# A two-stage attention kernel on one core: order of the first loads, staging of the weights, and projections of the first batch summed pair by pair

## The chip, the core and the metric

The kernel runs on one core of a Trainium2 chip. The engines are PE (TensorE, matrix products), DVE (VectorE), ACT (ScalarE), POOL (GpSimd) and SP (SyncE, which here only issues transfers). Each engine works through its own list of instructions in the order in which the program was written out, and waits at an instruction until what it needs is there. Times are device microseconds (us) of one execution, from the first to the last instruction plus what lies around them.

## What is computed

For 8 batches with 8 heads, 576 positions and head size 64, the reference adds two attentions and feeds the sum to a gated attention over four experts:

```
q_d, k_d, v_d = means over 4 neighbouring positions
out_up = repeat(softmax(scale * q_d @ k_d.T) @ v_d, 4)
scores = where(|i - j| < 4, scale * q @ k.T, -1e9)
x = out_up + softmax(scores) @ v              # (8, 576, 512)
logits = x @ w_gate ; keep the best 2 of 4 experts, softmax over them -> w
for e in range(4):
    q, k, v = x @ wq[e], x @ wk[e], x @ wv[e]
    ye = causal_softmax(scale * q @ k.T) @ v @ wo[e]
    out += w[e] * ye
```

## The kernel before

**Stages.** Heads are taken in pairs, four pairs to a batch, 32 pairs in all; pair 0 is the first of batch 0. Stage 1 makes x for one pair. Pair by pair it loads `lq`, `lk`, `lr` (v in rows of four positions) and `lv` (v in windows, two halves). PE makes the banded scores `sc` and the small scores `scd`. DVE masks (`lp`), takes the maximum, POOL subtracts it (L494; for a few pairs, list `LU`, ACT does this inside ten exponentials), ACT takes the exponential, DVE sums and inverts, POOL normalizes (L500). Means of four are `qd` and `kd` (L514, on DVE in batch 0) and `vd` (POOL, from `lr`, L528 and L529). PE transposes (`tp`), multiplies with v (`o`), DVE adds into `x` (L614), ACT rounds it to `xh` (L618), and POOL takes the rest `xl` (L619, and L621 for the last 64 positions).

**Stage 2** projects x of all four pairs: `q` and `k` of two halves of the experts (`pj`, L636) and five tiles of `v` with the gate (`pv`). Each product is three products of rounded parts (high by high, low by high, high by low), so one projection of `q` is, for each of the four pairs, three matmuls of 320 and three of 256 columns, and one tile of `v` is twelve matmuls of 260 columns. All four pairs add into the same sum. **Stage 3** makes scores (`sq`, `sqt`), softmax, transposes (`tq`), the product with v (`o`, L873) and the output product (`po`).

**Weights.** `weights()` loads `wqk` (1 MB), `wvg` (0.5 MB) and `wo` (0.5 MB), each into a staging tile `wst`, and splits them in chunks on ACT (high part, L434) and POOL or DVE (low part, L436). All three staging tiles have one buffer, so each load waits until the one before is split.

**Order.** A planner inside the kernel writes out the order. Every operation has a due time (its unit's place in a cycle of length `CYC`, less a lead by kind, `LEAD` and `OPL`, less `SHIFT`), a cost and its dependences; a model of the engines then takes, engine by engine, what is ready and due first. The order so found is fixed in the program. `WAT` holds the due times of the weights, `LDS` the lead of the loads. Where the model sees PE too idle, it puts in filler matmuls on constants (`wu`, `wub`, L444) that keep PE's clock up. 14 such matmuls (`NW0`) open the program.

Sums live in two pools of PSUM: two large buffers (`big`: `sc`, `o1`, `pj`, `po`, `sqt`) and four small ones (`tr`: `scd`, `tp`, `pv`, `sq`, `tq`).

In the model every projection depends on one object `WTS`, which stands for all the weights together:

```
xs = [(XH[b, c], 0) for c in range(NP)] + [XL[b, c] for c in range(NP)] + [WTS]
op(kind, "T", dense(12, 320), lambda: mm(0, 320), r=xs, w=[ps], alloc=[ps] + alloc)
```

Of the kernel before, what the change touches and what calls it, by code (L numbers as in the profile page):

```python
# [57 lines left out]
class Plan:  # L58
# [44 lines left out]
    def schedule(self):  # L103
# [17 lines left out]
        idle_at = dict(zip("TVAGD", (1069 + 427.0 * NW0, 4300.0, 2000.0, 1500.0, 300.0)))  # L121
# [162 lines left out]
SWM = {None: 16.3, "quarter": 14.0, "column": 36.7, "row": 12.3}  # L284
# [15 lines left out]
LAT = {"T": 200.0, "V": 130.0, "A": 150.0, "G": 150.0, "D": 2250.0}  # L300
# [15 lines left out]
def tile_attn_then_moe(ctx: ExitStack, tc: tile.TileContext, qT, kT, v, wqk, wvg, wo, out):  # L316
# [108 lines left out]
    def weights():  # L425
        for at, (src, n, m, whi, wlo) in zip(WAT, ((wqk, NP, 512, wqk_h, wqk_l), (wvg, NP, 260, wvg_h, wvg_l),
                                                   (wo, 2, D, wo_h, wo_l))):
            plan.now = at
            st = buf(wk, [128, n, m], "wst", NPA, tag="pta")
            op("wld", "D", 1500 if m == 260 else 2900, lambda st=st, src=src: nc.sync.dma_start(  # L430
                st(), src.rearrange("(c p) j -> p c j", p=128)), w=[st], alloc=[st])
            for c in range(n):
# [5 lines left out]
                   r=[(st, c)], w=[(WTS, key)])  # L438

# [12 lines left out]
    def load(b, c):  # L452
# [4 lines left out]
        op("load", "D", 830, lambda: nc.sync.dma_start(q(), qT[b, c]), w=[q], alloc=[q])  # L457
        op("load", "D", 830, lambda: nc.sync.dma_start(k(), kT[b, c]), w=[k], alloc=[k])
        op("load", "D", 830, lambda: nc.sync.dma_start(vr(), bass.AP(
            tensor=v.tensor, offset=v.offset + ((b * NP + c) * SP + PADL) * 128,  # L460
            ap=[[512, WD], [WD * 512, 2], [128, 4], [1, 128]])), w=[vr], alloc=[vr])
        for x, r in enumerate(halves):
            op("load", "D", 450, lambda x=x, r=r: nc.sync.dma_start(vw()[r], bass.AP(
                tensor=v.tensor, offset=v.offset + ((b * NP + c) * SP + SH * x) * 128,
                ap=[[128, W], [TQ * 128, 5], [1, 128]])), w=[(vw, x)], alloc=[] if x else [vw])

    def s1_local(b, c):
# [13 lines left out]
        op("local", "T", 600, mm, r=[q, k], w=[sc], alloc=[sc, p])  # L481
# [22 lines left out]
    def s1_down(b, c):  # L504
# [34 lines left out]
        op("down", "T", 500, mm, r=[qd, kd], w=scs, alloc=scs + [p])  # L539
# [28 lines left out]
    def s1_out(b, c):  # L568
# [60 lines left out]
    def project(kind, b, p, w0, alloc):  # L629
# [42 lines left out]
    def s2_v(b, t):  # L672
# [73 lines left out]
    def s2_scores(b, p, i):  # L746
# [15 lines left out]
        op("scores", "T", dense(3, n) + 20, mm, r=[q, k], w=pss, alloc=pss + [pr])  # L762
# [266 lines left out]
```

## Time and profile before

| | |
|---|---|
| runs: median (lowest to highest, 3 runs) | 541.54 us (540.61 to 543.1) |
| profiled execution, its span | 543.61 us, 541.8 us |
| PE busy | 515.7 us (95%) |
| DVE busy | 421.2 us (78%) |
| ACT busy | 330.5 us (61%) |
| POOL busy | 291.0 us (54%) |
| mean granted PE clock | 0.981 |

The span runs from the first to the last instruction. PE busy includes the fillers. The shares are averages over the whole run; the first 60 us look quite different from the rest.

### The profile page before, as it was taken

To read this page: it belongs to the slowest core of one execution; us is meant where nothing else is said; L and a number is where in the kernel's file an instruction comes from. 1 tells how busy PE (TensorE), PEld (TensorE's weight loads), DVE (VectorE), ACT (ScalarE), POOL (GpSimd) and SP (SyncE) were. 2 spreads that over 40 slices of the span, in tenths; PEclk is the share of its full clock that TensorE was granted. 3 is DMA by queue.
4 is the path that set the end of the run, shared out by engine and by line. 5 is a ranking of instruction groups with operands and counts; after the bars stand their busy time and mean duration, and the time that the engine had idled before them with its cause. 6 is when DMAs were issued, how large, how long until landed. Compare 5 with 4: busy or idle time off the path is not lost.

```text
span 541.8 us, 17296 instructions
## 1 busy us (share of the span) xinstructions
PE 515.7 (95%) x6870; PEld 453.5 (84%) x6872; DVE 421.2 (78%) x1256; ACT 330.5 (61%) x995; POOL 291.0 (54%) x360
## 2 busy tenths in 40 slices
PE   7596998999899999999999999999999999999998
PEld 3374898888789888999889998999988989998877
DVE  6597778879977879888789878896897796637871
ACT  1594663666556665676656566775665665545773
POOL 3397985737444656676534546865663653312220
PEclk8798999899999999999999999999999999999999
DMA  9868542603142323614144332632333010200112
GB/s 198 236 152 221 142 113 73 148 23 100 50 135 90 93 57 92 218 48 136 30 138 122 97 80 79 211 93 69 104 90 126 13 36 2 88 2 10 45 45 89
DMA packets 43585, 52.78 MB, mean 97 GB/s; under 512 B 3312, under 2 KB 26352, under 8 KB 43504
## 3 DMA queue, kind: packets, MB, share of 16 engines
q1 hardware_dynamic: 43504, 51.67, 34.0%
q8 instruction: 54, 0.88, 0.7%
q14 instruction: 27, 0.22, 0.1%
HBM read 41.16 MB, written 9.44 MB: 93 GB/s over the span
## 4 chain that ended last, share of the span: by engine, by line
PE 68%; DVE 14%; DMA 8%; ACT 4%; POOL 3%; issue 2%; SPq 1%; POOLq 0%; DVEq 0%; ACTq 0%
PE pj L636 14%; PE tq L827 7%; PE po L890 7%; PE o L873 7%; PE pv L681 7%; PE sq L761 6%; PE tp L578 6%; DMA lk<-in_kT_dram 4%; PE sc L479 3%; PE o L593 3%; PE o L607 2%; PE sqt L791 2%; DMA lq<-in_qT_dram 2%; PE scd L537 2%; DVE pr L776 1%
## 5 line engine op out<-in xcount | busy, mean ns | idle before, releaser
L767 ACT ACTIVATE pr<-pr,pst 128x512 f32<-128x512 f32 (+3 forms) x128 | 70.9, 555 | 27.1 <-DVE pst L769 25.6
L776 POOL TENSOR_SCALAR pr<-pr,pst,gw 128x256 f32<-128x256 f32 (+3 forms) x66 | 45.5, 692 | 66.3 <-DVE pst L774 34.3
L636 PE MATMUL pj<-xh,wqk_h 128*128 128x320 f32 (+1 forms) x256 | 79.6, 311 | 0.0
L636 PE MATMUL pj<-xl,wqk_h 128*128 128x320 f32 (+1 forms) x256 | 75.5, 295 | 0.0
L636 PE MATMUL pj<-xh,wqk_l 128*128 128x320 f32 (+1 forms) x256 | 75.4, 295 | 0.0
L769 DVE CUSTOM_DVE_ANT_0 pr<-sq,causal 128x512 f32<-128x512 f32 (+3 forms) x128 | 57.5, 484 | 11.2 <-PE sq L761 10.8
L827 PE MATMUL tq<-ident,pr 128*128 128x128 f32 x400 | 58.7, 276 | 4.7 <-DVE pst L769 1.4
L500 POOL TENSOR_TENSOR lp<-lp,lst 128x640 f32<-128x640 f32 x30 | 38.6, 1287 | 33.7 <-DVE lst L499 23.6
L827 PEld LDWEIGHTS tq<-ident,pr 128*128 128x128 f32 x400 | 45.3, 141 | 10.1 <-POOL pr L776 2.6
L636 PEld LDWEIGHTS pj<-xh,wqk_h 128*128 128x128 f32 x256 | 48.3, 189 | 1.3 <-issue 0.4
L636 PEld LDWEIGHTS pj<-xh,wqk_l 128*128 128x128 f32 x256 | 48.3, 189 | 0.0
L636 PEld LDWEIGHTS pj<-xl,wqk_h 128*128 128x128 f32 x256 | 48.1, 188 | 0.0
L549 ACT ACTIVATE dp<-scd,dst 128x144 f32<-128x144 f32 x96 | 35.2, 375 | 16.3 <-DVE dst L544 14.1
L761 PE MATMUL sq<-k,q 64*128 64x128 f32 (+3 forms) x384 | 43.4, 342 | 0.0
L528 POOL TENSOR_TENSOR lr<-lr 72x512 f32<-72x512 f32 x30 | 38.6, 1286 | 8.0 <-DMA lr<-in_v_dram 8.0
L619 POOL TENSOR_TENSOR xl<-x,xh 128x576 fp32r<-128x576 f32 x29 | 41.1, 1418 | 0.0
L353 DVE COPY pt<-tp 128x256 f32<-128x256 f32 (+2 forms) x64 | 31.8, 509 | 10.4 <-PE tp L578 10.1
L593 PE MATMUL o<-pt,lv 64*64 64x58 f32 (+1 forms) x1280 | 36.8, 229 | 2.2 <-DVE pst L793 1.8
L681 PE MATMUL pv<-wvg_h,xh 128*128 128x260 f32 x128 | 38.2, 298 | 0.0
L776 DVE TENSOR_SCALAR pr<-pr,pst,gw 128x256 f32<-128x256 f32 (+3 forms) x62 | 36.5, 593 | 0.7
L494 POOL TENSOR_TENSOR lp<-lp,lst 128x640 f32<-128x640 f32 x24 | 30.8, 1285 | 10.6 <-DVE lst L485 7.6
L890 PE MATMUL po<-oh,wo_h 128*128 128x320 f32 (+1 forms) x112 | 36.1, 322 | 0.3 <-DVE lp L482 0.3
(154 smaller groups left out, 1503.7 us busy)
## 6 DMA issues: line engine op xcount, KB each, us to landing
lv<-in_v_dram SPq DMA_DIRECT2D x64, 160.0 KB
lq<-in_qT_dram SPq DMA_DIRECT2D x32, 292.0 KB
lk<-in_kT_dram SPq DMA_DIRECT2D x32, 292.0 KB
lr<-in_v_dram SPq DMA_DIRECT2D x32, 288.0 KB
out_dram<-ot SPq DMA_DIRECT2D x28, 288.0 KB
wst<-in_wqk_dram SPq DMA_DIRECT2D x1, 1024.0 KB
out_dram<-ot SPq DMA_DIRECT2D x4, 160.0 KB
wst<-in_wvg_dram SPq DMA_DIRECT2D x1, 520.0 KB
```

What stands on the lines that cost most here:

```text
L500: op("l_nrm", "GV", (pool_tt(n), dve(n)), lambda e: eng[e].tensor_tensor(p(), p(), st[:, :, 2:3].to_broadcast([128, NT, W]), op=OP.mult), ...
L528: G.tensor_tensor(vr()[:, :, 0:2, :], vr()[:, :, 0:2, :], vr()[:, :, 2:4, :], op=OP.add)
L593: T.matmul(o()[r, 512 * x + z:512 * x + z + n], lv()[kr, t, r], pt()[kr, t - k0, at:at + n], start=True, stop=True)
L619: op("xl", "GV", (1360, dve(576)), lambda e: eng[e].tensor_tensor(xl(), x(), xh()[:, 0:S].bitcast(F32), op=OP.subtract), r=[x, (xh, 0)], w ...
L636: T.matmul(ps()[:, H0 + n0:H0 + n1], ww[:, c, w0 + 128 * p:w0 + 128 * p + 128], xx[b, c]()[:, n0:n1], start=(i == 0), stop=(i == 3 * NP - 1))
L681: T.matmul(ps()[:, :260], xx[b, c]()[:, 128 * t:128 * t + 128], ww[:, c, :], start=(i == 0), stop=(i == 3 * NP - 1))
L761: T.matmul(pss[e]()[:m, :n], q()[r, x, qc], k()[r, y, :n], start=one, stop=end)
L767: A.activation(pr()[:, e, :], pr()[:, e, :], AF.Exp, bias=st[:m, e, 4:5], scale=-1.0, accum_out=st[:m, e, 0:1])
L769: op("s_max", "V", dve(n) + 4, lambda e=e, ps=ps: V.tensor_tensor_reduce(pr()[:, e, :], ps()[:m, :n], causal[:, 640 - n:640], -0.125, BIG, ...
L776: op("s_nrm", "GV", (327 + n / 1.2, 189 + n / 1.92), lambda g, e=e: eng[g].tensor_scalar(pr()[:, e, :], pr()[:, e, :], st[:m, e, 3:4], gw( ...
L827: T.transpose(ps()[:, 128 * x:128 * x + 128], pr()[:, c] if i == 4 else pr()[:, e, c], ident)
L890: T.matmul(ps()[:, H0 + n0:H0 + n1], ww[:, p, 128 * c:128 * c + 128], xx[b, p]()[:, n0:n1], start=(i == 0), stop=(i == 5))
```

## The change

It does five things. Loads and weights of the first batch get another order: the loads of all four pairs first, `wvg` next, `wqk` after it, `wo` last (`WAT`, and a later due time `LVL` for the loads of `lv`). Each weight gets a staging buffer of its own, in space whose owner is not in use yet. A projection depends on its own weight, and chunk by chunk where it can. The first `q` projection and two `v` tiles of batch 0 are written as four parts, one for each pair, that add into a sum left open between them. The planner's numbers (due times, leads, some costs) are other ones, which moves instructions all through the program.

```
-CYC = 68.4
+CYC = 66.8
-WAT, NW0 = (36.0, 29.0, 58.0), 14
+WAT, NW0 = (48.0, 21.0, 52.0), 14
-LU, B0 = (1, 3, 8, 10, 16, 25, 26), 1
+LU, B0 = (1, 3, 8, 11, 14, 24, 26, 30), 1
-LDS = 5.8
+LDS, LVL = 5.2, 21.0
+PAIRWISE, NV1 = (("q", 0, 0),), 2
...
-            st = buf(wk, [128, n, m], "wst", NPA, tag="pta")
-            op("wld", "D", 1500 if m == 260 else 2900, lambda st=st, src=src: nc.sync.dma_start(
+            tag, bufs = {id(wqk): ("pta", NPA), id(wvg): ("ptb", NPB), id(wo): ("pr3", NPR[3])}[id(src)]
+            st = buf(wk, [128, n, m], "wst", bufs, tag=tag)
+            op("wld", "D", 2300 if m == 260 else 875 * n, lambda st=st, src=src: nc.sync.dma_start(
...
+    def needs(whi):
+        return [(WTS, (id(whi), c)) for c in range(whi.shape[1])]
...
+        plan.now += LVL
         for x, r in enumerate(halves):
-            op("load", "D", 450, lambda x=x, r=r: nc.sync.dma_start(vw()[r], bass.AP(
+            op("load", "D", 1150, lambda x=x, r=r: nc.sync.dma_start(vw()[r], bass.AP(
...
-        xs = [(XH[b, c], 0) for c in range(NP)] + [XL[b, c] for c in range(NP)] + [WTS]
+        xs = [(XH[b, c], 0) for c in range(NP)] + [XL[b, c] for c in range(NP)] + needs(wqk_h)
...
+    def project_by_pair(kind, b, p, w0, alloc):
+
+        ps = big("pj")
+
+        def mm(c):
+            for n0, n1 in ((0, 320), (320, S)):
+                for i, (ww, xx) in enumerate(((wqk_h, XH), (wqk_l, XH), (wqk_h, XL))):
+                    T.matmul(ps()[:, H0 + n0:H0 + n1], ww[:, c, w0 + 128 * p:w0 + 128 * p + 128], xx[b, c]()[:, n0:n1],
+                             start=(c == 0 and i == 0), stop=(c == NP - 1 and i == 2))
+        for c in range(NP):
+            op(kind, "T", dense(3, 320) + dense(3, 256) + 15, lambda c=c: mm(c), r=[(XH[b, c], 0), XL[b, c]] + needs(wqk_h)[c:c + 1],
+               w=[ps], alloc=[] if c else [ps] + alloc)
+        return ps
...
-            op("v", "T", dense(12, 260), mm, r=[(x, 0) for x in xh] + [XL[b, c] for c in range(NP)] + [WTS], w=[ps],
-               alloc=[ps] + ([vg] if t == 0 else []))
+            parts = [(c,) for c in range(NP)] if b == 0 and t < NV1 else [tuple(range(NP))]
+            for cs in parts:
+                op("v", "T", dense(3 * len(cs), 260) + 15, lambda cs=cs: mm(cs),
+                   r=[(xh[c], 0) for c in cs] + [XL[b, c] for c in cs] + [needs(wvg_h)[c] for c in cs], w=[ps],
+                   alloc=[ps] + ([vg] if t == 0 else []) if cs[0] == 0 else [])
```

What the planner makes of it is seen in the engines' lists. SP issues the transfers one after the other. Before, from its eighth transfer (numbers tell buffers apart; `lv_173` belongs to pair 1, `lq_248` to pair 2):

```order
L463 DMA lv_157<-in_v_dram 64x5x128
L463 DMA lv_173<-in_v_dram 64x5x128
L430 DMA wst_177<-in_wqk_dram 128x4x512
L463 DMA lv_173<-in_v_dram 64x5x128
L457 DMA lq_248<-in_qT_dram 128x584
L458 DMA lk_261<-in_kT_dram 128x584
```

And in the changed kernel from the same place (`lq_212` is pair 2, `lq_284` pair 3):

```order
L471 DMA lv_157<-in_v_dram 64x5x128
L464 DMA lq_212<-in_qT_dram 128x584
L465 DMA lk_241<-in_kT_dram 128x584
L466 DMA lr_257<-in_v_dram 72x2x512
L471 DMA lv_276<-in_v_dram 64x5x128
L464 DMA lq_284<-in_qT_dram 128x584
L465 DMA lk_319<-in_kT_dram 128x584
L466 DMA lr_335<-in_v_dram 72x2x512
```

The 1 MB of `wqk` stood ahead of the loads of pair 2; now those of pairs 2 and 3 come directly, `wvg` is the 17th transfer and `wqk` the 21st.

POOL's list before, around the last pair of batch 0 (`xl_874` is pair 2, `xl_971` pair 3, `lp_534` pair 4):

```order
L619 TENSOR_TENSOR xl_874<-x_745,xh_777 128x576
L500 TENSOR_TENSOR lp_534<-lp_534,lst1_73 128x640
L528 TENSOR_TENSOR lr_563<-lr_563 72x2x256
L529 TENSOR_TENSOR vd_903<-lr_563 72x256
L621 TENSOR_TENSOR xh_905<-x_893,xh_905 128x64
L619 TENSOR_TENSOR xl_971<-x_893,xh_905 128x576
L436 TENSOR_TENSOR wo_l_150<-wst_872,wo_h_149 128x512 x2
```

In the changed kernel (`lp_426` and `xl_895` are pair 3, `xl_828` pair 2, `lp_606` pair 4):

```order
L508 TENSOR_TENSOR lp_426<-lp_426,lst0_72 128x640
L440 TENSOR_TENSOR wqk_l_146<-wst_491,wqk_h_145 128x512 x3
L629 TENSOR_TENSOR xh_770<-x_743,xh_770 128x64
L440 TENSOR_TENSOR wqk_l_146<-wst_491,wqk_h_145 128x512
L627 TENSOR_TENSOR xl_828<-x_743,xh_770 128x576
L440 TENSOR_TENSOR wo_l_150<-wst_641,wo_h_149 128x512 x2
L629 TENSOR_TENSOR xh_853<-x_850,xh_853 128x64
L627 TENSOR_TENSOR xl_895<-x_850,xh_853 128x576
L502 TENSOR_TENSOR lp_606<-lp_606,lst1_73 128x640
```

The split of `wqk` and that of `wo` now lie ahead of the last `xl` of batch 0; the work for pair 4 (`lr_563`, the normalization of `lp_534`) went behind it.

On PE the first `q` projection before stands behind stage 1 of five pairs and some fillers:

```order
L607 MATMUL o1_948<-pt_999,vd_903 64x48 x2
L444 LDWEIGHTS causal_94
L444 MATMUL wu_1022<-causal_94 128x512
L444 LDWEIGHTS causal_94
L444 MATMUL wu_1028<-causal_94 128x512
L444 LDWEIGHTS causal_94
L444 MATMUL wu_1032<-causal_94 128x512
L636 MATMUL pj_1036<-xh_485,wqk_h_145 128x320
L636 MATMUL pj_1036<-xh_485,wqk_l_146 128x320
L636 MATMUL pj_1036<-xl_561,wqk_h_145 128x320
```

In the changed kernel the same projection (`pj_751`) begins between the transposes of pair 3:

```order
L586 MATMUL tp_746<-ident_115,lp_426 128x128 x2
L659 MATMUL pj_751<-xh_480,wqk_h_145 128x320
L659 MATMUL pj_751<-xh_480,wqk_l_146 128x320
L659 MATMUL pj_751<-xl_514,wqk_h_145 128x320
L659 MATMUL pj_751<-xh_480,wqk_h_145 128x256
L659 MATMUL pj_751<-xh_480,wqk_l_146 128x256
L659 MATMUL pj_751<-xl_514,wqk_h_145 128x256
L586 MATMUL tp_766<-ident_115,dp_645 72x128 x3
L586 MATMUL tp_773<-ident_115,dp_645 72x128 x3
L659 MATMUL pj_751<-xh_604,wqk_h_145 128x320
L659 MATMUL pj_751<-xh_604,wqk_l_146 128x320
L659 MATMUL pj_751<-xl_628,wqk_h_145 128x320
```

Its part for pair 2 follows after `o` of pair 3, that for pair 3 after the whole fifth `v` tile and `sc` of pair 6. Fillers behind the 14 at the start fall from 42 to 36.

## Rows read from the trace of the kernel before

**Rows 1.** Page: the span.

```profile
span 541.8 us, 17296 instructions
```

**Rows 2.** Windows: busy us (x instructions) of each engine, PE clock, DMA share, GB/s.

```profile
0.00:59.00 59.00, 43.92 (x785) 28.65 (x787) 44.40 (x114) 31.61 (x106) 37.48 (x55) 0.88 0.81 202
120.00:140.00 20.00, 19.03 (x286) 16.59 (x282) 18.07 (x59) 13.34 (x45) 11.14 (x14) 1.00 0.30 86
140.00:520.00 380.00, 375.35 (x4890) 339.44 (x4886) 301.86 (x922) 236.99 (x701) 197.15 (x240) 1.00 0.28 83
```

**Rows 3.** Timeline 0 to 32: start, us, engine, instruction [idle before <-releaser].

```profile
2.93 0.60 SPq L457 DMA_DIRECT2D lq<-in_qT_dram  x1
...
5.82 0.62 SPq L430 DMA_DIRECT2D wst<-in_wqk_dram  x1
...
8.04 0.51 SPq L457 DMA_DIRECT2D lq<-in_qT_dram  x1
...
8.74 0.75 DVE L514 TENSOR_REDUCE qd<-lq 128x144 f32<-128x576 f32 x1 [2.47 <-DMA lq<-in_qT_dram]
...
19.84 0.75 DVE L514 TENSOR_REDUCE qd<-lq 128x144 f32<-128x576 f32 x1 [2.55 <-DMA lq<-in_qT_dram]
...
20.70 0.61 ACT L434 CAST wqk_h<-wst 128x512 fp32r<-128x512 f32 x1
...
22.52 1.27 POOL L500 TENSOR_TENSOR lp<-lp,lst 128x640 f32<-128x640 f32 x1 [6.86 <-DVE lst L499]
```

**Rows 4.** Timeline 32 to 59: the last pair of batch 0.

```profile
45.59 1.34 ACT L434 CAST wvg_h<-wst 128x260 fp32r<-128x260 f32 x4 [4.05 <-DMA wst<-in_wvg_dram]
...
56.14 1.41 POOL L619 TENSOR_TENSOR xl<-x,xh 128x576 fp32r<-128x576 f32 x1
...
58.84 0.50 PE L636 MATMUL pj<-xh,wqk_h 128*128 128x320 f32 x1
```

**Rows 5.** Timeline 0 to 32: `sc`, mask, maximum and sum of pair 0.

```profile
7.17 0.81 PE L479 MATMUL sc<-lk,lq 64*64 64x64 f32 x40
...
11.08 0.81 DVE L482 SCALAR_TENSOR_TENSOR lp<-sc,lmask 128x640 f32<-128x640 f32 x1
...
12.18 0.81 DVE L485 TENSOR_REDUCE lst<-lp 128x10 f32<-128x640 f32 x1
...
16.46 0.82 DVE L497 TENSOR_REDUCE lst<-lp 128x10 f32<-128x640 f32 x1 [0.88 <-ACT lp L496]
```

**Rows 6.** Windows as in group 2: POOL's pass over batch 0, and one pair on PE.

```profile
22.50:57.60 35.10, 29.01 (x620) 21.17 (x614) 30.16 (x70) 21.97 (x73) 29.10 (x30) 0.88 0.72 184
53.90:58.40 4.50, 4.34 (x120) 3.60 (x122) 4.50 (x11) 3.27 (x11) 4.42 (x5) 1.00 0.70 205
```

**Rows 7.** Groups on POOL, 0 to 90: instruction, shape, count | busy us, mean ns | idle before.

```profile
L500 POOL TENSOR_TENSOR lp<-lp,lst 128x640 f32<-128x640 f32 x9 | 11.5, 1277 | 10.3 <-DVE lst L499 8.2 <-ACT up L612 2.0
L528 POOL TENSOR_TENSOR lr<-lr 72x512 f32<-72x512 f32 x9 | 11.5, 1277 | 8.0 <-DMA lr<-in_v_dram 8.0
...
L529 POOL TENSOR_TENSOR vd<-lr 72x256 f32<-72x256 f32 x9 | 6.5, 726 | 1.3 <-PE o L607 0.7
...
L436 POOL TENSOR_TENSOR wo_l<-wst,wo_h 128x512 fp32r<-128x512 f32 x2 | 2.5, 1288 | 0.0
```

**Rows 8.** Chain that ended last: start, us, what; projections on PE.

```profile
77.22 1.45 PE pv L681 x12
78.67 0.95 PE pv L690 x8
...
83.48 1.44 PE pj L636 x12
...
102.64 1.76 PE pj L636 x12
```

**Rows 9.** Windows as in group 2: around PE's longest wait after 59 us.

```profile
89.40:91.20 1.80, 0.03 (x4) 0.04 (x4) 1.76 (x7) 0.27 (x2) 0.58 (x1) 1.00 0.00 0
92.90:98.60 5.70, 5.70 (x132) 4.83 (x129) 4.20 (x14) 3.32 (x13) 4.66 (x6) 0.50 0.39 106
```

More of the change, by code (lines that the diff above doesn't have):

```diff
@@ L299 @@
         "GA": 75.0, "GT": 127.0}
-LAT = {"T": 200.0, "V": 130.0, "A": 150.0, "G": 150.0, "D": 2250.0}
+LAT = {"T": 200.0, "V": 130.0, "A": 150.0, "G": 150.0, "D": 2900.0}
 def dve(n):
@@ L675, in s2_v, with mm @@
         vg, ps = VG[b], small("pv")
-        def mm():
-            i = 0
-            for c in range(NP):
+        def mm(cs):
+            i = 3 * cs[0]
+            for c in cs:
                 for xx, ww in ((XH, wvg_h), (XH, wvg_l), (XL, wvg_h)):
@@ L761, in mm @@
                     T.matmul(pss[e]()[:m, :n], q()[r, x, qc], k()[r, y, :n], start=one, stop=end)
-        op("scores", "T", dense(3, n) + 20, mm, r=[q, k], w=pss, alloc=pss + [pr])
+        op("scores", "T", dense(3, n) + 100, mm, r=[q, k], w=pss, alloc=pss + [pr])
         for e in range(2):
@@ L791, in mm @@
                     T.matmul(dst, z[:, x, :], k()[:, y, n0:n1], start=one, stop=end)
-        op("tail", "T", dense(3, 320) + dense(3, 256), mm, r=[k, QZ[p % NQZ]], w=[ps], alloc=[ps, pr])
+        op("tail", "T", dense(3, 320) + dense(3, 256) + 90, mm, r=[k, QZ[p % NQZ]], w=[ps], alloc=[ps, pr])
         op("s_max", "V", dve(S) + 4, lambda: V.tensor_tensor_reduce(
@@ L916, in mm @@
                     i += 1
-        op("wo", "T", cost, mm, r=[(x[b, p], n0) for x in (OH, OL) for p in range(2)] + [WTS], w=[ps],
+        op("wo", "T", cost, mm, r=[(x[b, p], n0) for x in (OH, OL) for p in range(2)] + needs(wo_h), w=[ps],
            alloc=[ps] + ([ot] if one else []))
         op("wo_ev", "AV", (act(n), dve(n)), lambda e: copy(e, ot()[:, n0:n1], ps()[:, 0:n]), r=[ps], w=[(ot, n0)])
-        op("st", "D", 900, lambda: nc.sync.dma_start(out[b, 128 * c:128 * c + 128, n0:n1], ot()[:, n0:n1]),
+        op("st", "D", 1000, lambda: nc.sync.dma_start(out[b, 128 * c:128 * c + 128, n0:n1], ot()[:, n0:n1]),
            r=[(ot, n0)])
@@ L941, in stage3 @@
         last = b == B - 1
-        cuts = {ORD[2]: (CUT, S, 2010), ORD[4]: (0, CUT, 640)} if last else {2: (0, 384, 1270), 4: (384, S, 1380)}
+        cuts = {ORD[2]: (CUT, S, 2060), ORD[4]: (0, CUT, 690)} if last else {2: (0, 384, 1310), 4: (384, S, 1455)}
         sched = [(p, i) for p in range(2) for i in order(b)]
```

42 lines of the change are left out of this document (22 added, 20 removed).

## The prediction

> **What bounds the kernel now.** I first read the windows, to see where PE is not at work. Up to 59 us it is busy 43.9 us, fillers included, at a mean granted clock of 0.88; between 140 and 520 us it is busy 375.35 of 380 us at full clock [rows 2]. So from about 59 us on PE sets the pace and wastes almost nothing, and before that it waits for stage 1 of the first batch. The end comes earlier only by as much as PE's dense work starts earlier, or by what PE has already done at that point.
>
> The timeline shows what the first batch waits for. The 1 MB load of `wqk` is issued at 5.82. The `lq` load of pair 2, issued at 8.04, lets DVE go on only at 19.84; the second `lq` load, with nothing so large ahead of it, was issued at 2.93 and was there at 8.74 [rows 3]. DVE works in order, so the inversion for pair 0 stood behind this wait, and POOL, which idled 6.86 us for it, normalized pair 0 only at 22.52 [rows 3]. Later ACT stood 4.05 us before the first split of `wvg`, whose load had waited for the staging tile [rows 4]. The last `xl` of batch 0 ends at 56.14 + 1.41 = 57.55 and the first `pj` comes at 58.84 [rows 4].
>
> **The change, part by part.** The sum follows POOL from the normalization of pair 0 to the last `xl` of batch 0.
>
> *Start.* In the changed list `lq` of pair 2 is the ninth transfer, with no weight ahead of it. Its buffer still comes free around 8.04. If it takes as long as the second `lq`, 5.81 us, it is there at 13.85. Pair 0 itself is earlier too: DVE now has the mask of pair 0 directly behind `qd` and `kd` of pair 0, where the means of pair 1 stood between. `sc` of pair 0 ends at 7.98; from the start of the mask to the end of the maximum there were 12.99 - 11.08 = 1.91 us, and from there to the end of the sum 17.28 - 12.99 = 4.29 us [rows 5]. That gives 8.1 + 1.91 + 4.29 = 14.3. Behind it come two small steps for `scd` and `dst`, the mean `qd` of pair 2 (0.75) and the inversion, together about 1.7 us, an estimate. POOL can normalize pair 0 at 16.0 instead of 22.52: 6.5 us. Bounds: if `lq` of pair 2 still lands at 19.84, the start is at about 20.9 and the gain 1.6; if nothing waits, the start is at 15.
>
> *POOL's pass.* Between 22.5 and 57.6 POOL was busy 29.1 us and idle 6.0 [rows 6]. From this pass go one normalization and one subtraction (the same shape; 1.28 each), one `lr` (1.28) and one `vd` (0.73), all of pair 4 or later; two splits of `wo` (1.29 each) come in [rows 7]. Net 29.1 - 4.57 + 2.58 = 27.1 us. The idle time in it I leave at 6.0, though its causes differ. The wait for `wvg` should go: `wqk` was there 14.9 us after its issue at the latest, when ACT began to split it at 20.70 [rows 3]; `wvg` is half as large, is issued at about 14 by the same counting, and so lands near 21.5, ahead of its first split at about 25.5. New waits come: `wqk` is issued only when `lv` of pair 2 has a buffer, about 21.5, and with its 14.9 us it would land at 36, some 3 us after ACT gets to it. POOL also waits for `up`, `x` and `xh` of the last pairs, which DVE and ACT make. Bounds of the idle time: 0 and 12. So the last `xl` ends at 16.0 + 27.1 + 6.0 = 49.1 instead of 57.55: 8.45 us.
>
> *From the last `xl` to PE.* Before, 1.29 us passed, with three fillers in them. Now the last part of `q` waits at the head of PE's list, 0.2 us by my estimate: 1.1 us.
>
> *Work already done on PE.* A `q` projection costs 1.76 + 1.44 = 3.2 us, a `v` tile 1.45 us, the fifth tile 0.95 us [rows 8]. Ahead of the last part lie three parts of `q` (3 x 0.80), six parts of `v` (6 x 0.36) and the fifth tile: 5.5 us. Not yet done, and done before, is stage 1 of one pair (one each of `sc`, `scd`, both transposes, both products), which is what PE did in 4.34 us [rows 6]. Net 1.2 us.
>
> *Edits at nothing.* The parts are the same 24 matmuls of `q` and 12 for each tile of `v`, with the same weight loads. The other staging space belongs to tiles of stage 3, first written long after the split of `wo`, which ends about 47; if that cover were gone, a first transpose copy would wait for it. Fillers fall from 42 to 36, in time in which PE waits anyway. The open sums keep one of two `big` and two of four `tr` buffers from about 30 us until the last part; behind them queue `sc` of pairs 5 and 6, which wait for `x` of pair 3. DVE then lacks their masks for some us, and stage 1 of batch 1 is later, which is the second case below. The new order of all later batches I cost at nothing: PE idles only 4.65 us in 380 there, so little can be won.
>
> *Sum.* 8.45 + 1.1 + 1.2 = 10.75 us. The profiled execution took 543.61 us with a span of 541.8 [rows 1]; less the sum that is 532.9, and as it lay 2.1 above the median, 530.8. I say 531.
>
> **The rivals.**
>
> *The head is won, a part is lost behind it.* After the last `xl` POOL's list has two subtractions, two `lr`, two `vd` and then the normalization of pair 4: 3 x 1.28 + 2 x 2.0 = 7.85 us, so `tp` of pair 4 can start at about 57. PE's ready work until there is the rest of `q` and `v` (0.8 + 0.7), `k` (3.2) and two `v` tiles (2.9): 7.6 us, to 56.9. That is even, with no reserve, and pairs 4 and 5 then follow each other with little dense work between them. Say PE idles 3 us there. Before, an idle stretch of 1.78 us was followed by 5.7 us in which the granted clock was 0.50, its lower level [rows 9], which costs half of that, 2.85 us. Together 5.85: 537. [...]
>
> *More is won.* In that idle stretch DVE was busy 1.76 of 1.8 us [rows 9], with the ranking of the gate and what it had held up. In the changed list PE has the second `k` projection and stage 1 of another pair to do meanwhile. If the idle time and the slow stretch behind it go, 1.78 + 2.85 = 4.6 us more: 526.5.
>
> *No change.* The transfers may be the limit, whatever their order. If `lq` of pair 2 lands as late as before, the start wins 1.6 instead of 6.5, and if `wqk` at 36 also costs 3, what stays is 10.75 - 4.9 - 3 = 2.85, near the edge of what can be told from nothing: 539. Against it speaks that pair 1's loads were quick.
>
> *Slower.* Not the head but the other seven batches: all are reordered. If PE idled everywhere as between 120 and 140 us, 0.97 of 20 us or 4.85% [rows 2], that would be 18.4 us in 380 instead of 4.65, 13.8 more, and the time 544.5. It decides from 15.4 us of idle time on, 4.1%. Against it: every engine keeps its amount of work, and DVE was busy only 302 of those 380 us [rows 2].
>
> **How the numbers follow.** Forecast (528 to 534.5) 0.54, part lost (534.5 to 538.8) 0.22, more won 0.12, no change 0.07, slower 0.05. About 0.5%, 2.7 us, is what a measurement of this kernel can tell from no change, so "same" is 538.8 to 544.2. Faster: the first three, less a little of the second whose losses could be larger: 0.86. Same: 0.08. Slower: 0.06. The range takes in the bounds of the start and of the idle time as far as the first three cases and half of the fourth reach: 525.5 to 539.5.
>
> **What would show it.** In the changed profile POOL's first normalization stands at about 16, DVE's `qd` of pair 2 before 16, the last `xl` of batch 0 ends at 49 and the last part of `q` follows at once, and ACT has no wait of over 2 us for `wvg` or `wqk`. Between 57 and 70 PE idles under 3 us. From 140 us on PE is over 98% busy. The prediction is wrong if `lq` of pair 2 lands near 20, if POOL's pass has over 10 us of idle time, if pairs 4 and 5 hold PE up by more than 5 us, or if PE's idle time from 140 us on is three times what it was.

## The result and the profile after

The changed kernel took 536.33 us (median of 11 runs, 534.16 to 539.15) beside 541.54 us for the kernel before, a ratio of 0.991 with an interval of 0.9882 to 0.9938. A second set of runs on another chip gave 535.30 us and 0.9885 (0.9849 to 0.9921). So it is faster by about 1%, 5 to 6 us, where 10.5 were forecast. The time lies in the range (525.5 to 539.5), nearest to the case "the head is won, a part is lost behind it" (537), but most of the loss was not where that case put it.

The windows of the changed kernel (its profiled execution took 538.06 us, span 536.3; the columns are those of [rows 2]):

```profile
0.00:59.00 59.00, 47.14 (x733) 34.48 (x736) 42.84 (x110) 33.93 (x111) 41.00 (x58) 0.91 0.84 198
59.00:75.00 16.00, 16.00 (x303) 14.55 (x302) 12.14 (x32) 11.25 (x35) 13.98 (x17) 1.00 0.54 144
75.00:100.00 25.00, 21.95 (x382) 19.07 (x383) 24.12 (x76) 17.48 (x58) 20.17 (x25) 1.00 0.47 124
100.00:140.00 40.00, 39.38 (x477) 35.20 (x474) 30.97 (x96) 26.63 (x80) 20.10 (x25) 1.00 0.25 67
140.00:520.00 380.00, 372.12 (x4868) 336.18 (x4867) 304.96 (x934) 243.50 (x727) 187.99 (x224) 1.00 0.28 84
```

Against [rows 2] PE is busy 47.14 instead of 43.92 us by 59 us. But it idles 3.05 us between 75 and 100, where DVE is busy 24.12 of 25 us, and 7.88 instead of 4.65 us between 140 and 520. Two of PE's longest waits in each of these stretches, from its timeline (start, duration, and in brackets the idle time ahead and what ended it):

```profile
82.12 0.85 PE L586 MATMUL tp<-ident,dp 128*72 128x128 f32 x6 [0.80 <-ACT pt L354]
84.42 0.57 PE L601 MATMUL o<-pt,lv 64*64 64x58 f32 x24 [1.45 <-DVE x L622]
368.43 0.63 PE L852 MATMUL tq<-ident,pr 128*128 128x128 f32 x4 [1.29 <-DVE dst L552]
389.76 0.57 PE L601 MATMUL o<-pt,lv 64*64 64x58 f32 x24 [1.24 <-DVE pst L818]
```

The head, from the timelines of POOL and PE: the first normalization (22.52 in [rows 3]), the last `xl` of batch 0, the last part of `q` and the first transpose of pair 4.

```profile
17.31 1.27 POOL L508 TENSOR_TENSOR lp<-lp,lst 128x640 f32<-128x640 f32 x1 [2.05 <-DVE lst L507]
49.91 1.41 POOL L627 TENSOR_TENSOR xl<-x,xh 128x576 fp32r<-128x576 f32 x1
```
```profile
54.21 0.42 PE L659 MATMUL pj<-xh,wqk_h 128*128 128x320 f32 x1
61.92 0.71 PE L586 MATMUL tp<-ident,lp 128*128 128x128 f32 x5
```

Waits alone don't add up to the time, because a matmul at half clock counts as busy: from 46.46 to 52.9 us the granted clock is 0.51 and PE is busy all 6.44 us. So I measured how far PE is: every matmul but the fillers counts with the mean time that its kind takes from 140 us on, and the table gives, for the moment at which PE has done so much of its 487.5 us of work, how far a kernel is ahead of the profiled execution of the kernel before (us; the last two columns are experiments told below).

```
work done   changed   changed, second run   late order of before
 20           8.7        9.7                  9.5
 40           7.5       10.6                 10.4
 60           8.4       11.6                 11.4
120          11.3       14.5                 14.2
320          11.8       15.0                 13.6
360           8.0       11.2                 12.5
400           7.7       10.9                 12.6
487           6.8        9.9                 11.8
```

This is the main reading. Up to 60 us of work the lead is 7.5 to 8.7 us in one execution and 9.7 to 11.6 in the other, beside a forecast sum of 10.75. It grows by 3 more until 120. Between 320 and 400 of work, which in the profile is 357 to 443 us, about 4 of it are lost. Behind the last row of the table another 1.2 go: 4.5 us from there to the end of the span instead of 3.3.

The late loss goes with the late order in every trace of this case. Counted in this way, the changed kernel's two executions and the six experiments that keep its late order lose 4.0 to 4.1 us between 320 and 400. The two that keep it but for the ranking of batch 5 lose 3.2 and 3.4, and the three with the late order of the kernel before lose 0.9 to 1.0.

Of these 4.1 us some 3.2 are more idle time of PE (3.7 us between these two points, 0.6 before); in the rest its matmuls take longer than their kind does on average. The two longest waits, 1.29 and 1.24 us, are the last two rows of PE above. What happens ahead of them is on DVE and POOL, here from their timelines in the changed kernel:

```profile
365.01 1.51 DVE L801 TENSOR_SCALAR pr<-pr,pst,gw 128x256 f32<-128x256 f32 x1
366.44 1.30 DVE L629 TENSOR_TENSOR xh<-x,xh 128x64 fp32r<-128x64 f32 x1
384.19 1.71 DVE L744 TENSOR_TENSOR cm<-vg 128x80 f32<-128x80 f32 x1
385.82 1.32 DVE L745 TENSOR_TENSOR cm<-vg 128x80 f32<-128x80 f32 x1
```
```profile
364.94 1.43 POOL L627 TENSOR_TENSOR xl<-x,xh 128x576 fp32r<-128x576 f32 x1 [0.71 <-ACT xh L626]
366.33 1.33 POOL L502 TENSOR_TENSOR lp<-lp,lst 128x640 f32<-128x640 f32 x1
384.52 1.27 POOL L502 TENSOR_TENSOR lp<-lp,lst 128x640 f32<-128x640 f32 x1
385.76 1.28 POOL L536 TENSOR_TENSOR lr<-lr 72x512 f32<-72x512 f32 x1
```

Each of the four DVE operations ends within 0.2 us of a POOL operation's end (365.01 + 1.51 = 366.52, POOL 366.37; 385.82 + 1.32 = 387.14, POOL 387.04). The same two `cm` comparisons took 0.24 and 0.23 us in a run where POOL was idle (below). Against the shortest times of the same forms in this trace (0.40, 0.21, 0.21 and 0.23 us) about 4.8 us of these 5.8 are waiting, and the chain of waits runs through DVE from 361.4 to 368.4 and, but for one piece on ACT, from 376.3 to 392.9, so PE waits too. What in the hardware holds these operations until POOL's have ended, no run shows.

### The profile page after: what moved, and what is told of

Read it like the earlier page. It is cut to its first block, busy times and chain, and to the rows that moved or that the text cites. A ratio compares the mean times of both kernels' runs of the same rounds, so it can differ in the third digit from the quotient of the medians.

```text
span 536.3 us, 17270 instructions
## 1 busy us (share of the span) xinstructions
PE 511.0 (95%) x6864; PEld 450.7 (84%) x6866; DVE 418.0 (78%) x1251; ACT 338.9 (63%) x1026; POOL 284.4 (53%) x347
## 4 chain that ended last, share of the span: by engine, by line
PE 70%; DVE 16%; DMA 6%; POOL 3%; ACT 2%; issue 2%; SPq 1%; POOLq 0%; ACTq 0%; DVEq 0%
PE pj L644 14%; PE pv L703 8%; PE po L915 8%; PE o L898 8%; PE tq L852 7%; PE tp L586 5%; PE sq L786 5%; DMA lk<-in_kT_dram 4%; PE sc L487 3%; DVE pr L794 3%; PE o L601 3%; PE sqt L816 2%; PE o L615 2%; POOL pr L801 2%; PE scd L545 2%; DMA wst<-in_wqk_dram 2%
## 5 line engine op out<-in xcount | busy, mean ns | idle before, releaser
L801 POOL TENSOR_SCALAR pr<-pr,pst,gw 128x384 f32<-128x384 f32 (+3 forms) x70 | 51.8, 742 | 78.7 <-DVE pst L799 41.1
L644 PE MATMUL pj<-xh,wqk_h 128*128 128x320 f32 (+1 forms) x248 | 77.9, 314 | 0.1
L644 PE MATMUL pj<-xl,wqk_h 128*128 128x320 f32 (+1 forms) x248 | 73.2, 295 | 0.0
L644 PE MATMUL pj<-xh,wqk_l 128*128 128x320 f32 (+1 forms) x248 | 73.1, 295 | 0.0
L536 POOL TENSOR_TENSOR lr<-lr 72x512 f32<-72x512 f32 x32 | 40.9, 1277 | 8.0 <-DMA lr<-in_v_dram 7.6
L537 POOL TENSOR_TENSOR vd<-lr 72x256 f32<-72x256 f32 x32 | 23.4, 730 | 40.8 <-PE o L615 39.2
L508 POOL TENSOR_TENSOR lp<-lp,lst 128x640 f32<-128x640 f32 x28 | 35.8, 1278 | 12.5 <-DVE lst L507 10.8
L627 POOL TENSOR_TENSOR xl<-x,xh 128x576 fp32r<-128x576 f32 x27 | 38.4, 1422 | 1.5 <-ACT xh L626 1.5
L601 PE MATMUL o<-pt,lv 64*64 64x58 f32 (+1 forms) x1280 | 34.7, 224 | 4.7 <-DMA lv<-in_v_dram 2.0
L502 POOL TENSOR_TENSOR lp<-lp,lst 128x640 f32<-128x640 f32 x23 | 29.6, 1285 | 13.5 <-DVE lst L493 8.8
L601 PEld LDWEIGHTS o<-pt,lv 64*64 64x64 f32 x1280 | 27.2, 134 | 11.2 <-issue 2.9
```

The costliest lines, as they stand in the source:

```text
L536: G.tensor_tensor(vr()[:, :, 0:2, :], vr()[:, :, 0:2, :], vr()[:, :, 2:4, :], op=OP.add)
L601: T.matmul(o()[r, 512 * x + z:512 * x + z + n], lv()[kr, t, r], pt()[kr, t - k0, at:at + n], start=True, stop=True)
L627: op("xl", "GV", (1360, dve(576)), lambda e: eng[e].tensor_tensor(xl(), x(), xh()[:, 0:S].bitcast(F32), op=OP.subtract), r=[x, (xh, 0)], w ...
L644: T.matmul(ps()[:, H0 + n0:H0 + n1], ww[:, c, w0 + 128 * p:w0 + 128 * p + 128], xx[b, c]()[:, n0:n1], start=(i == 0), stop=(i == 3 * NP - 1))
L801: op("s_nrm", "GV", (327 + n / 1.2, 189 + n / 1.92), lambda g, e=e: eng[g].tensor_scalar(pr()[:, e, :], pr()[:, e, :], st[:m, e, 3:4], gw( ...
```

## The experiments

All are the changed kernel with an edit. Each operation carries a tag, and the list that the planner returned is edited (`seq`), so that everything else keeps its order; only for the late order the planner itself runs with other priorities. Lines up to 1000 are those of the changed kernel. Ratios are to the kernel before, run beside them on the same chip. The changed kernel was run on the first chip and on a second one, together with the staging tile alone, the last two together and the ranking of batch 5. All other kernels ran on two further chips without it, so they are compared with it by their ratios:

```
                                        median us (runs)  ratio   interval
changed, first                           536.33 (11)      0.9910  0.9882 to 0.9938
changed, again                           535.30 (6)       0.9885  0.9849 to 0.9921
no open sums                             539.98 (12)      1.0006  0.9971 to 1.0042
wqk staged in wvg's tile                 540.07 (10)      0.9982  0.9951 to 1.0013
both of these                            540.86 (12)      1.0018  0.9997 to 1.0039
wqk loaded ahead of pair 2               534.12 (6)       0.9896  0.9846 to 0.9946
late order of the kernel before          531.28 (6)       0.9838  0.9784 to 0.9893
the last two together                    531.06 (6)       0.9814  0.9786 to 0.9841
ranking of batch 5 moved                 534.59 (6)       0.9859  0.9816 to 0.9901
rankings of batches 0 and 5 moved        537.05 (7)       0.9925  0.9894 to 0.9955
late order, ranking of batch 0 moved     535.01 (7)       0.9905  0.9862 to 0.9948
eight more fillers                       537.77 (12)      0.9978  0.9939 to 1.0016
eight more fillers, again                536.96 (9)       0.9926  0.9888 to 0.9964
```

**The changed kernel again.** No edit.

> The changed kernel, not edited, once more, as the measure for the kernels beside it on this chip. In the trace that the comparison was read from, POOL's first normalization came at 17.3, later than in three other runs with the same order up to there (14.3, 15.1 and 15.3). Theory A (the head varies by some 2 to 3 us from execution to execution, the loss at 361 to 400 us does not): the first normalization comes at 14 to 16, PE is 14 us ahead of the kernel before at 275 us, and 3.5 to 4 us of that are gone at 400 us. Theory B (the loss at 361 to 400 us belongs to that one execution): PE keeps its lead to 500 us. Time 534 to 537 in either case.

POOL's first and last step of the head, and PE's first transpose of pair 4 and the late wait, from the timelines:

```profile
14.56 1.28 POOL L508 TENSOR_TENSOR lp<-lp,lst 128x640 f32<-128x640 f32 x1 [0.82 <-DVE lst L507]
42.69 0.32 POOL L629 TENSOR_TENSOR xh<-x,xh 128x64 fp32r<-128x64 f32 x1 [3.81 <-ACT xh L626]
48.70 1.44 POOL L627 TENSOR_TENSOR xl<-x,xh 128x576 fp32r<-128x576 f32 x1
```
```profile
58.77 0.71 PE L586 MATMUL tp<-ident,lp 128*128 128x128 f32 x5
386.58 0.57 PE L601 MATMUL o<-pt,lv 64*64 64x58 f32 x24 [1.27 <-DVE pst L818]
```

Theory A. The head differs from execution to execution with one and the same program (first normalization at 14.56 and 17.31); the late waits do not (1.29 and 1.24 us in the first trace, 1.29 and 1.27 at the same two instructions in the second). The lead table's second column is this run: 15.0 us at 320, 10.9 at 400.

**No open sums.**

```diff
+    for tag in (("q", 0, 0), ("v", 0, 0), ("v", 0, 1)):
+        parts = [o for o in seq if o.eng == "T" and o.tag == tag]
+        seq = [o for o in seq if o not in parts[:-1]]
+        at = seq.index(parts[-1])
+        seq[at:at] = parts[:-1]
```

> The changed kernel with one thing undone: the first three parts of the first q projection and of the two v tiles stand directly in front of the last part, so no sum is open and nothing of them is done ahead; every other instruction keeps its place. Theory A (PE is what limits the stretch behind the last xl, so work done ahead counts nearly in full): the 4.6 us of parts come after the last xl, the first tp of pair 4 moves from 61.9 to about 66, and the time rises by 4 to 5.5 us, to 540.5 to 542. Theory B (POOL's normalization of pair 4, which ended at 59.8, and the late batches limit, so that PE's work ahead is mostly slack): tp of pair 4 comes before 64 and the time rises by less than 2 us.

PE's timeline shows the four parts of `q` in a row, and `tp` of pair 4 3.65 us later than in the second run of the changed kernel:

```profile
49.33 0.63 PE L659 MATMUL pj<-xh,wqk_h 128*128 128x320 f32 x1
62.42 0.71 PE L586 MATMUL tp<-ident,lp 128*128 128x128 f32 x5
```

Theory A by the time: with 1.0006 the whole gain is gone, so the work done ahead counts nearly in full. `tp` itself came before 64, as theory B had said, and 3.65 us are little more than the 3.15 between the two executions of the changed kernel; the claim rests on the times.

**wqk staged in wvg's tile, and both parts undone.** The first moves the load of `wqk` behind the last split of `wvg` and gives both the same space; the load of `wo`, which stands behind it, is late with it. The second adds the edit above.

```diff
+    a, b = [o for o in seq if o.kind == "wld"][:2]
+    at = max(i for i, o in enumerate(seq) if o.kind in ("whi", "wlo") and a in o.deps) + 1
+    seq.insert(at, b)
+    seq.remove(b)
+    a.allocs[0].tag = "pta"
```

> The changed kernel with wqk staged in the tile that wvg uses, as the weights shared one before: the load of wqk is issued only when POOL has ended the splits of wvg, near 32.5 instead of 25.4, and wo's load behind it. Theory A (the staging tiles are what let the new order work): wqk lands near 40 instead of 35.1, POOL's splits of it start 4 to 5 us later, the last xl of batch 0 ends at 54 to 56 instead of 49 to 51, and the time rises by 3 to 5 us. Theory B (there is slack between wqk's landing and the last xl): the last xl moves by less than 2 us and the time by less than 1.5.

> The changed kernel with two of its parts undone at once: no open sums (4.8 us alone, against the same kernel before) and wqk staged in wvg's tile (4.8 us alone). The order of all other instructions stays the changed one. Theory A (they relieve two different waits, PE's work ahead and the arrival of wqk): the losses add, 543 to 545.5, slower than the kernel before. Theory B (both make the same thing earlier, the first dense work of PE): 540 to 542, no more than one of them alone.

ACT's first split of `wqk` (alone, without a wait, at 30.89 in the second run of the changed kernel) waits for the load. Then come POOL's last `xl` of batch 0 and windows further on, in which PE falls to half clock (the clock is the third number from the end):

```profile
36.33 0.62 ACT L438 CAST wqk_h<-wst 128x512 fp32r<-128x512 f32 x1 [4.86 <-DMA wst<-in_wqk_dram]
50.92 1.43 POOL L627 TENSOR_TENSOR xl<-x,xh 128x576 fp32r<-128x576 f32 x1
```
```profile
75.00:80.00 5.00, 5.00 (x93) 4.53 (x92) 4.93 (x15) 3.18 (x14) 4.32 (x7) 1.00 0.45 132
80.00:85.00 5.00, 2.85 (x40) 2.18 (x38) 4.79 (x19) 3.36 (x11) 1.45 (x3) 0.80 0.36 85
85.00:90.00 5.00, 5.00 (x94) 4.24 (x90) 3.73 (x12) 2.60 (x10) 3.63 (x5) 0.50 0.44 101
```

The time is as theory A said (0.9982, 4.8 us over the changed kernel), though the last `xl` ended only 2.2 us later, at 52.35. Another 3.3 us of lead go between 40 and 60 of work, where the slow stretch lies in this trace. It is not this execution alone: over all ten runs the mean granted clock was 0.984, beside 0.989 for the changed kernel on the same chip. Both together cost no more than one alone (1.0018): theory B, the losses do not add. That both bring the same first dense work forward is the reason theory B gives; the times show only that they overlap.

**wqk loaded ahead of pair 2.**

```diff
+    wld = min((o for o in seq if o.kind == "wld"), key=lambda o: o.seq)
+    seq.remove(wld)
+    seq.insert(next(i for i, o in enumerate(seq) if o.tag == ("load", 0, 2)), wld)
```

> The changed kernel with one thing undone: the load of wqk is issued in front of the loads of pair 2, as before the change; its own staging tile, all other loads and every other instruction keep their order. Theory A (the order of the loads made the earlier start): POOL's first normalization goes from 17.3 back to about 22, the last xl of batch 0 ends near 56 instead of 51.3, and the time rises by 4 to 5 us, to about 541. Theory B (the start was won by the staging tiles and by DVE's order, or what is won at the start is lost again behind it): the first normalization stays before 19, or it moves and the time rises by less than 1.5 us.

POOL's timeline:

```profile
19.38 1.28 POOL L508 TENSOR_TENSOR lp<-lp,lst 128x640 f32<-128x640 f32 x1 [4.94 <-DVE lst L507]
44.70 0.33 POOL L629 TENSOR_TENSOR xh<-x,xh 128x64 fp32r<-128x64 f32 x1
50.35 1.44 POOL L627 TENSOR_TENSOR xl<-x,xh 128x576 fp32r<-128x576 f32 x1
```

Theory A falls. POOL starts 4.8 us later and ends only 1.65 us later: the wait of 3.81 us for `xh` of pair 2 is gone, and the chain of waits runs through POOL without a stop from 30.3 to 47.6. With `wqk` in front POOL waits early, with `wqk` behind it waits in the middle. What it waits for there is not settled: in the first trace PE stands 1.20 us at 35.77 and 0.78 us at 44.17 for `lv`, in the second 2.35 us ahead of a `scd` at 35.69, for which the profile names no cause (first trace, then second):

```profile
35.77 0.56 PE L601 MATMUL o<-pt,lv 64*64 64x58 f32 x20 [1.20 <-DMA lv<-in_v_dram]
```
```profile
35.69 0.89 PE L545 MATMUL scd<-kd,qd 64*64 64x144 f32 x12 [2.35 <-issue]
```

The time shows no difference (0.9896 beside 0.9885 and 0.991); the upper end of its interval, 0.9946, excludes the 541 us of theory A. The place of this load in the list brings much of the early start that I had derived from it, but no time that can be told from nothing.

**The late order of the kernel before.** From 260 us of the planner's own time on, priorities are the places in the old list; `LU` mixes the two lists.

```diff
-LU, B0 = (1, 3, 8, 11, 14, 24, 26, 30), 1
+LU, B0 = (1, 3, 8, 11, 14, 16, 25, 26), 1
...
-            progress = True
+            progress, late = True, renumber(self, t)
...
+            at = LATE.get(k, ())
+            o.prio = at[n] if n < len(at) else 0.0
```

> The changed kernel up to about 275 us, where the trace has it 12 us ahead of the kernel before; from there on the planner takes the ready operations in the order in which they stood in the kernel before (the operations are the same; in three of the late pairs the subtraction is done as in the kernel before). Theory A (the head and the first batches won about 12 us, and the changed kernel's own late order gave 4 to 5 of them back, at 361 to 400 us, where DVE set the pace and waited 4.9 us for POOL): PE idles under 1 us between 355 and 400, and the time is 531 to 532, 4 to 5 us under the changed kernel. Theory B (whatever arrives earlier is given back, since DVE and POOL cannot go faster in any order): 535 to 537, no different from the changed kernel.

> Both together: the late order of the kernel before from about 275 us on (531.3 alone) and the load of wqk in front of pair 2's loads (534.1 alone, where the changed kernel would have been at about 535.3). Theory A (the place of the wqk load is worth nothing either way, as the last xl ends within 1 us of where it was): 531 within 1 us. Theory B (the early wqk load gains about 1 us on its own, since PE's pairwise parts of q come sooner and keep the clock up): 529.5 to 530.5.

The windows from 355 to 400 us, of the changed kernel and then of this one:

```profile
355.00:400.00 45.00, 42.08 (x644) 36.86 (x643) 36.65 (x113) 28.24 (x89) 21.43 (x24) 1.00 0.32 88
```
```profile
355.00:400.00 45.00, 43.81 (x598) 39.44 (x596) 37.16 (x115) 27.72 (x85) 26.36 (x32) 1.00 0.29 86
```

Theory A: 531.28 and, with `wqk` in front, 531.06. PE idles 1.19 instead of 2.92 us (a little over the 1 us expected), and from 320 to 400 of work 1.0 us of lead is lost, not 4.1. The old order is not better everywhere (from 120 to 320 it loses 0.6 where the changed one gains 0.5); it is better at that place and at the end, where it has the 3.3 us of the kernel before. With `wqk` in front the ratio is 0.9814 (0.9786 to 0.9841) beside 0.9896 (0.9846 to 0.9946) without the old order. What is not parted is the order and `LU`: in three late pairs the subtraction is done as in the kernel before, and no run changes that list alone. This is the fastest version.

**The ranking of batch 5 moved.**

```diff
+    rank = next(o for o in seq if o.kind == "g_rank" and o.tag == ("gate", 5))
+    exp = next(o for o in seq if o.kind == "g_exp" and o.tag == ("gate", 5))
+    tail = next(o for o in seq if o.kind == "s_max" and o.tag == ("scores", 5, 0, 4))
+    seq.remove(rank)
+    seq.remove(exp)
+    at = seq.index(tail) + 1
+    seq[at:at] = [rank, exp]
```

> The changed kernel with one move: the first part of the gate's ranking of batch 5 (seven small operations on DVE, at 384.2, two of which took 1.71 and 1.32 us where 0.2 is usual, each until a POOL operation ended) stands behind the copy of pt, the mean kd and the maximum of the tail scores, where POOL waits for PE. [...] Theory B (DVE is full there, in any order): the operations may be quick, but PE's lead at 400 us is the same within 0.5 us.

```profile
386.06 0.24 DVE L744 TENSOR_TENSOR cm<-vg 128x80 f32<-128x80 f32 x1
386.21 0.23 DVE L745 TENSOR_TENSOR cm<-vg 128x80 f32<-128x80 f32 x1
```
```profile
390.07 0.55 PE L786 MATMUL sq<-k,q 64*128 64x128 f32 x5 [0.67 <-DVE ol L904]
```

The same PE instruction in the changed kernel:

```profile
392.20 0.55 PE L786 MATMUL sq<-k,q 64*128 64x128 f32 x5 [0.19 <-DVE ol L904]
```

These rows of DVE and PE show it: 0.24 and 0.23 us instead of 1.71 and 1.32, the wait of 1.24 us is gone, but the next grows from 0.19 to 0.67. Moving these operations away from POOL's gave PE 0.8 us, and the loss between 320 and 400 of work is 3.2 instead of 4.1 us, a little more than theory B allowed. The intervals (ratios 0.9859 and 0.9885) overlap, so the time alone shows nothing. The other pair of stretched operations, ahead of the wait of 1.29 us at 368.43, was not moved by itself; that it is the cause there is read from the rows, not shown by an experiment.

**The ranking of batch 0 moved,** with that of batch 5, and with the late order.

```diff
+    ranks = [o for o in seq if o.tag == ("gate", 0)]
+    x = next(o for o in seq if o.kind == "x" and o.tag == ("out", 1, 2))
...
+    at = 1 + next(i for i, o in enumerate(seq) if i > seq.index(x) and o.kind == "tp_ev" and o.who == "V")
+    seq[at:at] = ranks[:2]
+    low = next(o for o in seq if o.kind == "k_lo" and o.tag == ("k", 0, 1))
+    seq.insert(seq.index(low) + 1, ranks[2])
```

> The changed kernel with the gate's ranking moved on DVE in two places: that of batch 5 as in the run that moved it alone, and that of batch 0, which stood at 74.3 to 80.4 in the second run of the changed kernel (two of its operations took 1.33 and 1.20 us beside POOL's) and now stands behind the addition x of pair 6 and one copy of pt, where POOL has a gap of 3.6 us. Theory A (DVE is the limit from 74 to 90 and its waits for POOL are avoidable): PE's waits of 0.79 and 1.44 us at 79 and 81 shrink to under 1 us together, and the time is 2 to 4 us under the changed kernel, 531.5 to 533.5. Theory B (DVE is busy 97 per cent of that stretch in any order, so the wait only moves): PE idles 2.5 us or more between 75 and 95 as before, and the time is within 1.5 us of the changed kernel.

> The version with the late order of the kernel before from about 275 us on (531.3), and with the ranking of batch 0 moved as in the kernel beside it. Theory A: both gains add, 529 to 530. Theory B (the first is real, the second only moves a wait): 531 to 532.

Neither brought the gain of its theory A, and in the second theory B's 531 to 532 was missed too. The first stands at 537.05, with 3.56 us of PE idle between 75 and 95, as its theory B had it (2.5 or more). PE's and DVE's rows of the second of them, and its window from 85 to 95 us:

```profile
81.01 0.81 PE L487 MATMUL sc<-lk,lq 64*64 64x64 f32 x40 [1.01 <-DVE k L670]
85.42 1.74 PE L786 MATMUL sq<-k,q 64*128 64x384 f32 x6 [2.27 <-DVE pst L794]
```
```profile
81.28 1.33 DVE L760 TENSOR_SCALAR gs<-gs 128x5 f32<-128x5 f32 x1
82.88 0.99 DVE L762 TENSOR_TENSOR gw<-gw,gs 128x20 f32<-128x20 f32 x1
```
```profile
85.00:95.00 10.00, 9.41 (x82) 7.91 (x83) 9.07 (x33) 7.59 (x25) 6.87 (x9) 0.66 0.28 73
```

The first half of the ranking now runs freely, but its second half falls beside POOL's next `xl`: 1.33 us for five elements per partition, which took 0.17 us with POOL idle (the run that moved batch 5's ranking alone). PE waits 3.28 us in two pieces, and idles 3.79 us between 75 and 95, against 3.01 in the second run of the changed kernel; behind the two waits the clock falls (1.00 in the window from 75 to 85, 0.66 from 85 to 95). So at this place the wait only moved, and grew: 0.9905 against 0.9838 for the late order without it, 3.6 us, though the intervals just overlap. The leads say the same: between 50 and 80 of work they fall by 2.2 and 3.2 us in the two traces with this ranking moved, and rise by 0.8 in the changed kernel and in the late order without the move.

**Eight more fillers,** in two places where PE had waited before its clock fell in the first trace.

```diff
+        if o.eng == "T" and o.kind == "down" and o.tag == ("down", 1, 1):
+            o.fn = lambda fn=o.fn, b=o.allocs[0]: [T.matmul(b()[:, :512], zero[:, :128], zero, start=True, stop=True)
+                                                  for _ in range(4)] and fn()
...
```

> The changed kernel with eight more filler matmuls on PE (four in front of the first product of pair 3 at 43.1, four in front of the scores of pair 5's means at 45.7), where PE waited 1.6 us for DVE and for a load before its clock fell to 0.50 from 46 to 52.9. Theory A (that slow stretch is a loss of the head): the granted clock stays 1.00 from 46 to 53, PE reaches tp of pair 4 1.5 to 2.5 us earlier than 61.9, and the time falls by 1.5 to 2.5 us, to about 534. Theory B (PE has slack there, since the last xl ends at 51.3 and the normalization of pair 4 at 59.8, or the clock falls anyway): within 0.7 us of the changed kernel.

> The kernel with eight more filler matmuls, not edited, on another chip: it was expected to be 1.5 to 2.5 us faster than the changed kernel and came out at 0.9978 of the kernel before, where the changed kernel stood at 0.9885 and 0.991. Theory A (fillers do nothing here, the difference was of that chip): 0.987 to 0.992 of the kernel before. Theory B (they cost time): 0.995 or more again.

No gain: 0.9978, and 0.9926 on another chip; the expected 1.5 to 2.5 us would be 0.984 to 0.988, under both intervals. In the trace of the first run the clock is 1.00 from 46 to 53 us, as theory A asked. But so it is in the second run of the changed kernel, without these fillers, and the mean granted clock over all runs (0.990 and 0.991) is that of the changed kernel (0.991 and 0.989). Neither theory of the second run is shown; that these fillers don't pay is.

## Why the prediction was off, step by step

*Start.* Said: 16.0. It was 17.3 in the compared trace and 14.3 to 16.1 in the eight other traces with this list of loads, and `qd` of pair 2 ran at 13.55 in the second run, 16.29 in the first. Right as a time; wrong as a gain. The 6.5 us did not reach the end of POOL's pass, since POOL then waited in the middle ("wqk loaded ahead of pair 2"). For the place of this load the rival "no change" was right in what it is worth, not in why: `lq` of pair 2 did come early.

*POOL's pass.* Busy 27.14 us in the first trace and 27.20 in the second, as the sum of rows had said (27.1). Idle 7.0 and 8.5 instead of 6.0, inside the bounds. The last `xl` ended at 51.3 and 50.1, said 49.1.

*From the last `xl` to PE.* Said: at once. It took 2.9 us in the first trace, where PE was at half clock from 46 to 52.9 and still had other parts to do, and 0.9 us in the second run. Such a slow stretch is the loss which the rival had put behind 57 us; pair 4's transposes waited for POOL in neither of the two traces. PE had waited 0.78 us until 44.17, and the clock fell within another wait of 0.81 us, which ended at 46.46 (0.71 in the window from 45.65 to 46.46, 0.50 in the one behind it). In the second run it fell behind the wait of 2.35 us that ended at 35.69, and the windows show 0.74 from 30 to 43 us. In the first trace the windows from 30 to 46 us, where the first small parts of `q` lie (40.61 and 42.09), show 1.00, so the parts as such do not bring the low clock.

*Work done ahead.* Right, and more important than I had it: without it nothing is left of the gain. The parts of `q` and `v` were priced at 4.6 us (3 x 0.80 and 6 x 0.36), and undoing them cost 5 to 6.5 us by the ratios. Net 1.2 us in the sum was small only because I had charged one pair of stage 1 against it.

*Head as a sum.* 10.75 us were forecast; the lead was 7.5 to 8.7 us in the first trace and 9.7 to 11.6 in the second. With the measured terms the sum would be 6.2 - 1.6 + 1.2 = 5.8 and 7.4 + 0.4 + 1.2 = 9.0, some 1.6 us under the leads at 40 of work. So the nearness of the second run is in part luck: less came from the last `xl` than was said, and 1.6 us that the sum does not have came on top.

*More is won.* It came, but elsewhere. Where it was looked for, the idle time grew from 1.78 to over 3 us while the half clock of [rows 9] went away, and the lead rose by only 0.9 to 1.0 us between 40 and 60 of work. It rose by 2.9 us between 60 and 120, where the kernel before waited in small pieces (0.97 us from 120 to 140 us [rows 2]) and the changed one idles 0.62 us in all of 100 to 140.

*The later batches at nothing.* This is the step that failed: "The new order of all later batches I cost at nothing: PE idles only 4.65 us in 380 there, so little can be won". Little could be won, but I did not ask what could be lost. About 4 us went between 357 and 443 us and 1.2 at the end; the old order from 275 us on gains 8.8 us on the kernel before beside it (531.28 against 540.12), and 10.1 with `wqk` in front (531.06 against 541.15), where 10.5 were forecast for the change as a whole. The rival "slower" had the right place, all later batches, but the wrong form: not idle time everywhere, but one place where DVE, with 113 operations in 45 us, stands behind POOL, and the end. My mark for it, three times the idle time, was too coarse: it rose by 1.7 times, and PE was busy 97.9% where I had asked for 98.

What is left open: the leads are against one profiled execution of the kernel before, which lay 2.1 us above its median. They give 8.7 us at the end of the span for the second run; the medians give 5.9. The 1.2 us at the end, which the late order of the kernel before gives back, are not traced to a cause. And whether a better place would free the ranking at 80 us from POOL was not tried.

## What to carry to other kernels

When a list scheduler reorders a whole program for an edit at its start, price the far part too: a stretch in which PE idles 1% has little to win and more to lose. Follow PE's lead in work done as well as its idle time; it shows where a gain is given back. And an earlier first step is worth only what the waits behind it let through: move it back alone, and see whether the end moves.

## What the runs showed of the hardware

In the rows above, DVE operations of five to eighty elements per partition took 0.99 to 1.71 us beside POOL operations of 1.27 to 1.42 us, and ended within 0.2 us of one; with POOL idle the same ones took 0.17 to 0.24 us. Summed over all DVE instructions as the excess over the lowest tenth of the same form, stretching of any cause is 30 us in both kernels. Some 14 us of it before and 17 in the changed kernel lie in operations at least 0.2 us over that end with a POOL operation. So the two kernels differ less in how much DVE is held up than in where.

The same program varies in its first 50 us: POOL's first normalization came at 14.56 or 17.31 and the half-clock stretch fell into 36 to 43 or 46 to 52.9 us, while from 140 us on two executions agree to 0.2 us of PE time (372.12 and 371.91 of 380).

The granted clock has two values in the traces of the kernel before and of the changed one, 1.00 and 0.50. What the fillers do for it is seen in the kernel before: PE ran nothing else from 12.82 to 16.15 us, and in that stretch the clock rose from 0.50 (the window from 12 to 12.75) to 1.00 (from 13.9 on). It was still 1.00 after the fillers at 35.28 and at 41.14, with waits of 0.76 and 1.26 us behind them, and fell to 0.50 within the wait of 5.46 us that ended at 21.60 and behind that of 2.67 us that ended at 47.82. Eight more fillers in the changed kernel brought no gain (0.9978 and 0.9926).
